# A windowed-attention and gated-MLP kernel on one core: VectorE takes values ahead of the next pair's mask, queries are turned between two output rows, later pairs are cast one slot sooner

## The chip, the core and the metric

The kernel runs on one core of a Trainium2 chip. A core has five engines that run side by side and meet only at semaphores: TensorE (PE in the profile; PEld is its weight load), VectorE (DVE), ScalarE (ACT), GpSimd (POOL) and SyncE (SP), which here only issues transfers. Each engine takes its instructions strictly in the order in which the program gives them. The metric is the device time of one execution in microseconds, the median of several runs.

## What is computed

Four batches, eight heads, 768 positions, head size 64. Attention with a window of 128 positions and four sink positions, then a gated MLP over the 512 joined head outputs, with a mixing over positions:

```python
scores = scale * np.matmul(q, k.transpose(0, 1, 3, 2))
is_sink = pos[None, :] < int(n_sink)
rel = pos[:, None] - pos[None, :]
in_window = (rel >= 0) & (rel < int(window))
scores = np.where(is_sink | in_window, scores, -1000000000.0)
a = np.exp(scores - np.max(scores, axis=-1, keepdims=True))
a = a / (np.sum(a, axis=-1, keepdims=True) + 1e-09)
x = np.matmul(a, v)            # then heads joined: (4, 768, 512)
...
h = x @ w_in                   # 512 -> 1024, then gelu (tanh form)
u, v = h[..., :512], h[..., 512:]
v_n = (v - mu) / np.sqrt(var + 1e-06) * g_ln
v_s = np.einsum('ts,bsd->btd', w_sg, v_n) + b_sg[None, :, None]
out = x + (u * v_s) @ w_out
```

## The kernel before

The work is cut into 16 pairs of heads (`n` = 0 to 15, four to a batch) and, behind each batch's four pairs, one MLP block. For a pair, `load` (L90) brings `k`, `q` and `v` from HBM, `cast` (L101) turns them to bf16 on GpSimd, and keys and queries are turned so that the head size lies on the partitions: `columns` (L215) does it by TensorE into PSUM with a copy out by ScalarE or VectorE, `columns_by_dma` (L228), for pairs 12 to 15, by transposing transfers on SP's queue.

`score(n, g)` (L251) computes the scores of group `g`, two of the six key tiles, in PSUM, and ScalarE's exponential writes them to `ex`. `keep_band` (L283) then zeroes what lies outside the window: for group 0 VectorE multiplies with a mask (L290), for groups 1 and 2 GpSimd runs two selects (L298, L300). `values(n, c)` (L307) multiplies half `c` of the pair's query tiles (three each) with the values and the sinks (L324, L330); VectorE then takes the reciprocal of the sums (L332) and the product that writes `x` (L333). `turn_x` (L337) turns `x` by TensorE, `turn_x_by_dma` (L352) by a transfer on SP.

The block of a batch is `hidden` (L577): six `hidden_v` units (L370, L377, gelu L379, statistics L381), eight `hidden_u` units (L389, L392), the inverse root, and the normalisation (L422). Steps of the next pair are placed between its units by unit number. What follows it in the MLP is put in the list `fillers`: eight gate units `spatial` (L424: six matmuls L432, then VectorE's L435 and L438) and six output rows `project` (L458: four matmuls L463; either VectorE adds `x` at L466, or a fifth matmul does at L469 and ScalarE copies at L472; then a store on SP). `fill()` takes the next unit off this list, so that TensorE has MLP work of the last batch between the attention steps of the next.

All PSUM tiles but the scores come from `bank` (L209), four buffers that go round: a tile waits until the tile four before it has been read out. Scores have two buffers of their own. The bf16 keys and queries have two buffers each, the raw loads three.

The order of all this is written by hand. For pairs 4 to 15 a loop (L701 to L760) writes it: slot `n` of the loop holds the scores and masks of pair `n`, the values of pair `n-1`, the turns of pair `n+1` and the casts of pair `n+2`, with conditions for the first slots, the last ones and those with a block (`block`, n = 8 and 12). In a slot, the mask of group 0 stands ahead of `values(n - 1, 0)`:

```python
        keep_band(n, 0, V)
        keep_band(n, 1, G)
        if n + 2 >= FIRST:
            cast_all(n + 2, "kq")
        if todo:
            values(n - 1, 0)
        fill(2 if n > HP and not todo else 1)
```

After a block no values of the pair before are left to do (`todo` is false), and the last thing placed inside it is `score(n + 1, 0, 1)` and two units of `fillers`. What follows the loop (from L761), the last pair's values and the last block, is the same in both kernels.

Of the kernel before, what the change touches and what calls it, by code (L numbers as in the profile page):

```python
# [18 lines left out]
def kernel(  # L19
# [14 lines left out]
    nc = tc.nc  # L34
# [317 lines left out]
    def turn_x_by_dma(n):  # L352
        b, hp = divmod(n, HP)
        nc.sync.dma_start_transpose(
            out=xT[b][:, hp, :].rearrange("c (t p) -> c t p", t=NT),
            in_=x_sb[b][:, hp].rearrange("p t c -> p (t c)"))
# [98 lines left out]
                A.copy(o_sb, o_ps[:, 0:m])  # L455
            (nc.sync if eng is V else A).dma_start(out=out[b, rows, cols], in_=o_sb)

    def project(b, t, by_act):  # L458
        rows = slice(128 * t, 128 * (t + 1))
        o_ps = bank([128, 512], F32, "o_ps")  # L460
        o_sb = small.tile([128, DM], F32, name="o_sb", bufs=6)
        for c in range(KU):
            nc.tensor.matmul(o_ps, gTs[b][:, c, rows], w_out_sb[:, c, :],  # L463
                             start=(c == 0), stop=(c == KU - 1 and not by_act))
        if not by_act:
            V.tensor_add(o_sb.rearrange("p (h d) -> p h d", h=HP),  # L466
                         o_ps.rearrange("p (h d) -> p h d", h=HP), x_sb[b][:, :, t, :])
        else:
            nc.tensor.matmul(o_ps.rearrange("p (h d) -> p h d", h=HP), iden, x_sb[b][:, :, t, :],  # L469
                             start=False, stop=True)  # L470
        if by_act:
            A.copy(o_sb, o_ps)  # L472
        nc.sync.dma_start(out=out[b, rows, :], in_=o_sb)


    LEAST, MOST = 1e-20, 1e20
# [95 lines left out]
    def fill(count=1):  # L572
        for _ in range(count):
            if fillers:
                fillers.pop(0)()

    def hidden(b, between):  # L577
        units = [lambda j=j: hidden_v(b, j) for j in range(NT)]
        units += [lambda f=f, n=n: hidden_u(b, f, n) for n in range(2) for f in range(KU)]
        after = {NT + 1: [lambda: inverse_root(b)]}  # L580
        for j in range(NT):
            after.setdefault(NT + 1 + j, []).append(lambda j=j: normalise(b, j))
        for i, unit in enumerate(units):
            unit()
            for step in after.get(i, []) + between.get(i, []):
                step()
        gate = [[lambda f=f, n=n: spatial(b, f, n) for f in range(KU)] for n in range(2)]
        if b < B - 1:
            fillers.extend(gate[0] + gate[1])
            order = (0, 2, 4, 1, 3, 5) if b < B - 2 else (1, 0, 2, 3, 4, 5)  # L590
            fillers.extend(lambda t=t: project(b, t, t % 2 == 1) for t in order)
# [98 lines left out]
    cast_all(HP + 1)  # L690
    load_w_out()

    QUOTA = {4: 3, 5: 3, 6: 3, 7: 2, 8: 1, 9: 3, 10: 3, 11: 3, 12: 3, 13: 3, 14: 3, 15: 3}
    LAST = NT + 2 * KU - 1

    def x_by_dma(n):
        return n >= 2 * HP and n % HP < HP - 2

    later = {2 * HP: (FIRST, FIRST + 1), 3 * HP: (NP - 1, NP)}
    valued = HP - 1  # L700
    for n in range(HP, NP):  # L701
        todo = valued < n - 1
        block = n % HP == 0 and n > HP
        if HP < n <= 2 * HP:
            load_all(n + 3)
        if n not in exps:
            score(n, 0, 1)
        if n == HP:
            for si in range(3, NT):
                turn_weights(si, V)  # L710
        keep_band(n, 0, V)
        keep_band(n, 1, G)
        if n + 2 >= FIRST:
            cast_all(n + 2, "kq")
        if todo:
            values(n - 1, 0)
        fill(2 if n > HP and not todo else 1)
        if n + 1 < FIRST and not block:
            columns(n + 1, "k", A)
            if not todo and n > HP:  # L720
                columns(n + 1, "q", V)
        if n == HP:
            columns(n + 1, "q", V)
            fill()
        score(n, 2)
        keep_band(n, 2, G)
        if todo:
            values(n - 1, 1)
            if x_by_dma(n - 1):
                turn_x_by_dma(n - 1)  # L730
        if FIRST <= n + 2 < NP:
            columns_by_dma(n + 2)
            if n + 4 == FIRST + 2:
                load_all(n + 4)
        if QUOTA[n] > 2 and todo:
            fill()
        if HP < n < FIRST - 1 and not block and todo:
            columns(n + 1, "q", A)
        if n + 2 <= NP:
            cast_all(n + 2, "v" if n + 2 >= FIRST else "kqv")  # L740
        if n == NP - 1:
            draw_gelu()
        if QUOTA[n] > 1:
            fill()
        if block:
            open_v(n // HP - 1, 0)
            open_v(n // HP - 1, 1)
        if todo and not x_by_dma(n - 1) and n < NP - 1:
            turn_x(n - 1, V)
        if block:  # L750
            open_v(n // HP - 1, 2)
        valued = n - 1
        if block:
            hidden(n // HP - 1, {1: [lambda: values(n, 0)], 3: [lambda: values(n, 1)],
                                 5: [lambda: columns(n + 1, "k", A)] if n + 1 < FIRST else [],
                                 6: [lambda m=m: load_all(m) for m in later.get(n, ())],
                                 7: [lambda: columns(n + 1, "q", A)] if n + 1 < FIRST else [],
                                 9: [lambda: turn_x_by_dma(n) if x_by_dma(n) else turn_x(n, V)],
                                 LAST: [lambda: score(n + 1, 0, 1), lambda: fill(2)]})
            valued = n  # L760
    values(NP - 1, 0)  # L761
    fill()
    turn_x(NP - 2, A)
# [51 lines left out]
```

## Time and profile before

| | us |
|---|---|
| median of 3 runs | 167.05 |
| the runs | 165.91, 167.05, 175.5 |
| profiled execution | 166.5 |
| its span, first to last instruction | 164.7 |
| TensorE busy | 153.1 |
| VectorE busy | 132.9 |
| ScalarE busy | 110.1 |
| GpSimd busy | 77.6 |

The span is what the profile's rows add up to; the profiled execution's own time has some 2 us around it. In rows of the timeline the columns are: start, length, engine, line, operation, output from inputs, count, and in brackets the idle time of the engine before it with what ended it. In rows of the chain of waits: start, length, engine and tile. The ends of matmuls are modelled, so overlapping lengths are usual there. The granted TensorE clock was full (0.991 in the mean).

The stages in time: pairs 0 to 3 to about 24 us, the first block to about 37, slots 4 to 8 to about 63.7, the second block to 76, slots 9 to 12 to 99.5, the third block to 111, slots 13 to 15 and the last pair's values to 130.7, then the last block, gate and rows.

### The profile page before, as it was taken

Reading aid. Unit: us, or ns where it says so; the run is one execution under the profiler, and the core shown is the slowest. Engines: PE = TensorE matmul, PEld = TensorE weight load, DVE = VectorE, ACT = ScalarE, POOL = GpSimd, SP = SyncE. Lnnn points to the kernel's source line nnn. Section 1 sums busy time; section 2 is a strip of 40 time slices with the busy share of each in tenths; the row PEclk is TensorE's granted clock in tenths of the full one; section 3 lists DMA queues with packets and bytes.
Section 4 is the critical chain, followed back from the end, with each engine's and each line's share of the span. In section 5 each row is a group of like instructions: output and inputs, shape, how many; then the busy total and the mean of one; then the engine's idle time right before and its main releaser. Section 6 shows DMA issues by size and latency. Waiting matters only on the chain.

```text
span 164.7 us, 4433 instructions
## 1 busy us (share of the span) xinstructions
PE 153.1 (93%) x1737; PEld 91.4 (55%) x1755; DVE 132.9 (81%) x321; ACT 110.1 (67%) x150; POOL 77.6 (47%) x113
## 2 busy tenths in 40 slices
PE   3999999999999999999999989999999999999950
PEld 3555574666566665564666645555565545455530
DVE  6787995996899986799889995989899869987520
ACT  3189878879978689698887466679759267411220
POOL 6568771207799989400289997000996000000000
PEclk9999999999999999999999999999999999999996
DMA  4999989999999999999902999999622310040361
GB/s 133 333 339 259 197 116 261 224 325 307 295 237 304 254 306 359 278 213 222 183 27 56 149 234 183 242 228 211 190 53 48 127 68 0 17 174 4 127 235 38
DMA packets 60195, 31.11 MB, mean 189 GB/s; under 512 B 48356, under 2 KB 57080, under 8 KB 60168
## 3 DMA queue, kind: packets, MB, share of 16 engines
q1 hardware_dynamic: 56800, 27.47, 70.5%
q0 software_dynamic: 2944, 2.77, 10.4%
q10 hardware_dynamic: 424, 0.53, 1.0%
q8 instruction: 15, 0.25, 0.6%
q14 instruction: 12, 0.10, 0.2%
HBM read 24.81 MB, written 6.29 MB: 189 GB/s over the span
## 4 chain that ended last, share of the span: by engine, by line
PE 68%; DVE 22%; issue 3%; ACT 2%; POOL 1%; DVEq 0%; ACTq 0%
PE vs L432 11%; PE hu L389 10%; PE o_ps L463 9%; PE hv L370 8%; PE sc L267 7%; PE av L324 6%; DVE gv L435 4%; DVE gT L438 3%; PE kps L219 3%; PE xps L341 3%; PE qps L219 2%; PE hv L377 2%; DVE st L381 2%; ACT ex L281 2%; PE av L330 2%
## 5 line engine op out<-in xcount | busy, mean ns | idle before, releaser
L281 ACT ACTIVATE ex<-sc 128x1024 bf16<-128x1024 f32 x48 | 47.5, 1025 | 11.8 <-PE sc L267 7.1
L432 PE MATMUL vs<-wsgT,vn 128*128 128x384 bf16 x192 | 35.3, 326 | 0.1
L298 POOL TENSOR_SCALAR_AFFINE_SELECT ex<-ex 128x512 bf16<-128x512 bf16 x24 | 16.8, 700 | 30.0 <-ACT ex L281 15.6
L463 PE MATMUL o_ps<-w_out_sb,gT 128*128 128x512 bf16 x83 | 22.9, 380 | 1.1 <-DVE x L333 0.6
L432 PEld LDWEIGHTS <-vn 128*128 128x128 bf16 x192 | 17.6, 98 | 10.8 <-DVE vn L422 0.2
L389 PE MATMUL hu<-xT,w_in_sb 128*128 128x384 bf16 x128 | 22.1, 326 | 0.0
L435 DVE SCALAR_TENSOR_TENSOR gv<-vs,g_sb,b_bc 128x384 bf16<-128x384 f32 x32 | 19.5, 610 | 2.5 <-PE vs L432 2.1
L381 DVE BATCH_NORM_STATS2 st<-v_all 128x6 f32<-128x512 f32 x24 | 16.1, 671 | 3.5 <-ACT v_all L379 3.5
L370 PE MATMUL hv<-w_in_sb,xT 128*128 128x512 bf16 x68 | 18.6, 379 | 0.3
L333 DVE TENSOR_TENSOR x<-av,rcps 128x384 bf16<-128x384 f32 x32 | 17.8, 558 | 1.1
L379 ACT ACTIVATE v_all<-hv 128x512 f32<-128x512 f32 x24 | 13.2, 599 | 7.8 <-PE hv L377 6.6
L392 ACT ACTIVATE uT<-hu 128x384 bf16<-128x384 f32 x32 | 15.7, 491 | 4.1 <-PE hu L389 3.7
L438 DVE TENSOR_TENSOR gT<-gv,uT 128x384 bf16<-128x384 bf16 x32 | 16.6, 517 | 2.2 <-DVE gv L435 0.5
L107 POOL CAST k_bf<-k_sb 128x768 bf16<-128x768 f32 x15 | 12.8, 853 | 11.1 <-DMA k_sb<-in_k_dram 5.8
L472 ACT COPY o_sb<-o_ps 128x512 f32<-128x512 f32 x13 | 7.4, 593 | 15.2 <-PE o_ps L469 7.5
L389 PEld LDWEIGHTS <-w_in_sb 128*128 128x128 bf16 x128 | 12.3, 98 | 8.0
L267 PE MATMUL sc<-qT,kT 64*128 64x256 bf16 (+2 forms) x384 | 16.0, 256 | 0.7 <-DVE qT L225 0.3
L107 POOL CAST q_bf<-q_sb 128x768 bf16<-128x768 f32 x15 | 14.4, 958 | 4.2 <-DMA q_sb<-in_q_dram 3.9
L324 PE MATMUL av<-v_sb,ex 128*128 128x65 bf16 x352 | 16.2, 194 | 0.0
L104 POOL CAST v_sb<-v_sb 128x768 bf16<-128x768 f32 x16 | 14.6, 911 | 3.0 <-DMA v_sb<-in_v_dram 2.9
L290 DVE TENSOR_TENSOR ex<-ex,mask 128x1024 bf16<-128x1024 bf16 x15 | 13.9, 925 | 2.5 <-ACT ex L281 2.3
L324 PEld LDWEIGHTS <-ex 128*128 128x128 bf16 x352 | 13.1, 97 | 4.7 <-issue 1.4
(90 smaller groups left out, 221.3 us busy)
## 6 DMA issues: line engine op xcount, KB each, us to landing
k_sb<-in_k_dram SPq DMA_DIRECT2D x16, 384.0 KB, 6.7
v_sb<-in_v_dram SPq DMA_DIRECT2D x16, 384.0 KB, 6.0
out_dram<-o_sb SPq DMA_DIRECT2D x23, 256.0 KB, 2.4
q_sb<-in_q_dram SPq DMA_DIRECT2D x15, 384.0 KB, 5.5
wsg_sb<-in_moe_w_sg_dram POOLq DMA_DIRECT2D x2, 576.0 KB, 11.3
w_in_sb<-in_moe_w_in_dram POOLq DMA_DIRECT2D x2, 256.0 KB, 5.1
w_in_sb<-in_moe_w_in_dram POOLq DMA_DIRECT2D x1, 512.0 KB, 5.4
w_out_sb<-in_moe_w_out_dram POOLq DMA_DIRECT2D x1, 512.0 KB, 9.2
```

The source lines that it names most:

```text
L107: eng.tensor_copy(dst.rearrange("p t (h d) -> p h t d", h=2), src)
L267: nc.tensor.matmul(sc[part, 512 * l + w:512 * l + w + n_q], kT[rows, 128 * j + wide * a:128 * j + wide * (a + 1)], qT[rows, 128 * j:128 * ...
L281: A.activation(out=exps[n][:, g, :], in_=sc, func=AF.Exp, scale=scale)
L324: nc.tensor.matmul(av[:, m, l, :], probs(j, l, half), v_sb[:, l, j, :], start=first, stop=False)
L333: V.tensor_mul(x_sb[b][:, hp, HT * c:HT * (c + 1), :].rearrange("p i (l d) -> p i l d", l=2), av[:, :, :, 0:64], rcp.to_broadcast([128, HT ...
L370: nc.tensor.matmul(hvs[b, j], xT[b][:, c, 128 * j:128 * (j + 1)], w_in_sb[:, c, DF:], start=(c == 0), stop=False)
L381: V.bn_stats(out=st, in_=v_alls[b][:, j, :])
L389: nc.tensor.matmul(h_ps[:, 0:NH], w_in_sb[:, c, 128 * f:128 * (f + 1)], xT[b][:, c, NH * n:NH * (n + 1)], start=(c == 0), stop=(c == KD - 1))
L432: nc.tensor.matmul(vs[:, 0:NH], vns[b][:, si, 128 * f:128 * (f + 1)], wsgT[:, si, cols], start=(si == 0), stop=(si == NT - 1))
L435: V.scalar_tensor_tensor(out=gv, in0=vs[:, 0:NH], scalar=g_sb[:, f:f + 1], in1=b_bc[:, cols], op0=ALU.mult, op1=ALU.add)
L438: V.tensor_mul(gTs[b][:, f, cols], gv, uTs[b][:, f, cols])
L463: nc.tensor.matmul(o_ps, gTs[b][:, c, rows], w_out_sb[:, c, :], start=(c == 0), stop=(c == KU - 1 and not by_act))
```

## The change

The loop is replaced by a list of steps in the order in which they are emitted. A letter names the function: `S` scores, `m` masks (`m 5 0 1`: groups 0 and 1 of pair 5), `A0`/`A1` the halves of `values`, `ck cq cv` casts, `KA QA KV QV` turns of keys or queries with the engine of the copy, `TD` turns by transfer, `XV XA XD` turns of `x`, `L` loads, `F` a unit of `fillers`, `W` weights, `O` the opening of `hidden_v`, `B` a block. Most of the list repeats the loop's order. What differs:

- In slots 5, 6, 7, 10, 11, 14 and 15, `A0` of the pair before stands ahead of the mask of group 0 (and of group 1, which runs on another engine).
- Slot 8: the mask of group 0 of pair 8 stands behind both halves of pair 7's values. The output row between them is split: its matmuls stay (`D`), its ScalarE copy and its store (`E`) come behind `A1`, and so behind the exponentials of group 2. `project` gets the argument `ends` for it.
- Slot 12: the mask of group 0 of pair 12 stands behind both halves of pair 11's values and the output row after them.
- Behind the second block: the queries of pair 10 are turned between the two output rows and not three units later; the casts of pair 11's keys and queries and pair 10's values stand ahead of pair 9's group 1 and 2 selects.
- The key and query casts of pairs 12, 13 and 14 stand at the end of slots 9, 10 and 11 and not between the selects of slots 10, 11 and 12; the key cast of pair 15 stands ahead of the selects of pair 13.

```diff
-    def project(b, t, by_act):
+    def project(b, t, by_act, ends=None):
...
-        if not by_act:
-            V.tensor_add(o_sb.rearrange("p (h d) -> p h d", h=HP),
-                         o_ps.rearrange("p (h d) -> p h d", h=HP), x_sb[b][:, :, t, :])
-        else:
+        if by_act:
             nc.tensor.matmul(o_ps.rearrange("p (h d) -> p h d", h=HP), iden, x_sb[b][:, :, t, :],
                              start=False, stop=True)
-        if by_act:
-            A.copy(o_sb, o_ps)
-        nc.sync.dma_start(out=out[b, rows, :], in_=o_sb)
+        def end():
+            if by_act:
+                A.copy(o_sb, o_ps)
+            else:
+                V.tensor_add(o_sb.rearrange("p (h d) -> p h d", h=HP),
+                             o_ps.rearrange("p (h d) -> p h d", h=HP), x_sb[b][:, :, t, :])
+            nc.sync.dma_start(out=out[b, rows, :], in_=o_sb)
+        if ends is None:
+            end()
+        else:
+            ends.append(end)
...
-    for n in range(HP, NP):
-        todo = valued < n - 1
-        block = n % HP == 0 and n > HP
...
+    INSIDE = {
+        1: {1: "A0 8", 3: "A1 8", 5: "KA 9", 6: "L 12, L 13", 7: "QA 9", 9: "XD 8",
+            LAST: "ck 11, cq 11, cv 10, S 9 0 1, F 1, QV 10, F 1"},
+        2: {1: "A0 12", 3: "A1 12", 6: "L 15, L 16", 9: "XD 12", LAST: "S 13 0 1, F 2"},
+    }
+    ORDER = """
+        S 4 0 1, W 3 4 5, m 4 0 1, F 1, KA 5, QV 5, F 1, S 4 2, m 4 2, ck 6, cq 6, cv 5, F 1,
+        L 8, S 5 0 1, A0 4, m 5 0 1, F 1, KA 6, S 5 2, m 5 2, A1 4, F 1, QA 6,
+        ck 7, cq 7, cv 6, F 1, XV 4,
+        L 9, S 6 0 1, A0 5, m 6 0 1, F 1, KA 7, S 6 2, m 6 2, A1 5, F 1, QA 7,
+        ck 8, cq 8, cv 7, F 1, XV 5,
+        L 10, S 7 0 1, A0 6, m 7 0 1, F 1, KA 8, S 7 2, m 7 2, A1 6, QA 8,
+        ck 9, cq 9, cv 8, F 1, XV 6,
+        L 11, S 8 0 1, A0 7, m 8 1, D, S 8 2, m 8 2, A1 7, E, m 8 0, ck 10, cq 10, cv 9,
+        O 1 0, O 1 1, XV 7, O 1 2, B 1,
+        m 9 0 1, F 1, KA 10, F 1, S 9 2, m 9 2, ck 12, cq 12, F 1,
+        S 10 0 1, A0 9, m 10 0 1, F 1, KA 11, S 10 2, m 10 2, A1 9, XD 9, TD 12, L 14,
+        F 1, QA 11, cv 11, ck 13, cq 13, F 1,
+        S 11 0 1, A0 10, m 11 0 1, F 1, S 11 2, m 11 2, A1 10, TD 13, F 1, cv 12, ck 14, cq 14,
+        F 1, XV 10,
+        S 12 0 1, A0 11, m 12 1, F 1, S 12 2, m 12 2, A1 11, TD 14, F 1, m 12 0, cv 13, F 1,
+        O 2 0, O 2 1, XV 11, O 2 2, B 2,
+        ck 15, m 13 0 1, cq 15, F 2, S 13 2, m 13 2, TD 15, cv 14, F 1,
+        S 14 0 1, A0 13, m 14 0 1, F 1, S 14 2, m 14 2, A1 13, XD 13, F 1, cv 15, F 1,
+        S 15 0 1, A0 14, m 15 0 1, F 1, S 15 2, m 15 2, A1 14, F 1, G, F 1
+    """
...
+    run(ORDER)
```

The function `run` only calls, for each letter, the function named above; `D` calls `fillers.pop(0)(ends)` and `E` calls `ends.pop()()`. The step `B` calls `hidden` with the entries of `INSIDE` as what is placed between its units.

More of the change, by code (lines that the diff above doesn't have):

```diff
@@ L589, in hidden @@
             fillers.extend(gate[0] + gate[1])
+            by_act = (1, 3, 5)
             order = (0, 2, 4, 1, 3, 5) if b < B - 2 else (1, 0, 2, 3, 4, 5)
-            fillers.extend(lambda t=t: project(b, t, t % 2 == 1) for t in order)
+            fillers.extend(lambda ends=None, t=t: project(b, t, t in by_act, ends) for t in order)
             return
@@ L691 @@
     load_w_out()
-    QUOTA = {4: 3, 5: 3, 6: 3, 7: 2, 8: 1, 9: 3, 10: 3, 11: 3, 12: 3, 13: 3, 14: 3, 15: 3}
     LAST = NT + 2 * KU - 1
[L696 to L700, printed above, removed]
-    for n in range(HP, NP):
-        todo = valued < n - 1
-        block = n % HP == 0 and n > HP
[L704 to L760, printed above, removed]
```

40 lines of the change are left out of this document (added).

## The prediction

> **What bounds the kernel now.** I read the page's busy shares and the shares of the chain of waits first, then the windows, then the timeline of every slot that the change touches.
>
> ```profile
> PE 153.1 (93%) x1737; PEld 91.4 (55%) x1755; DVE 132.9 (81%) x321; ACT 110.1 (67%) x150; POOL 77.6 (47%) x113
> PE 68%; DVE 22%; issue 3%; ACT 2%; POOL 1%; DVEq 0%; ACTq 0%
> 43.50:130.70 87.20, 85.63 (x1076) 51.97 (x1085) 77.17 (x182) 65.71 (x87) 54.50 (x77) 1.00 0.94 198
> ```
>
> TensorE carries the chain, VectorE takes it over for a fifth. The edits lie between 43.5 us (scores of pair 5) and 130.7 us (the last pair's values). The third row is that stretch: its length, then the busy time of PE, PEld, DVE, ACT and POOL. TensorE is idle there for 87.20 - 85.63 = 1.57 us. The change takes no matmul away and adds none, so what it can win is this idle time, and a little that the modelled ends of stalled matmuls hide: some 2 us in all, about 1.2% of 166.5 us. Before 43.5 us nothing changes; after 130.7 us the order is the old one and only shifts. The question is thus which stalls of TensorE go, one by one. In all that follows I compare the starts of successive matmul groups, since their ends are modelled.
>
> **Values ahead of the mask: slot 7.** In slots 5 to 7, 10, 11, 14 and 15 the reciprocal and product of `values(n-1, 0)` now stand ahead of the mask of pair n, group 0, on VectorE. No other engine's order changes by that. The PSUM tiles of `bank` go round in four buffers, so the product that empties one lets the fourth tile after it start. In slot 7 that tile is `qps` (queries of pair 8).
>
> ```profile
> 52.69 0.34 PE L330 MATMUL av<-vsink,ex 128*128 128x195 bf16 x2
> 52.90 0.50 PE L432 MATMUL vs<-wsgT,vn 128*128 128x384 bf16 x2
> ...
> 57.08 0.99 DVE L290 TENSOR_TENSOR ex<-ex,mask 128x1024 bf16<-128x1024 bf16 x1
> 58.21 0.56 DVE L333 TENSOR_TENSOR x<-av,rcps 128x384 bf16<-128x384 f32 x1
> 58.45 0.34 PE L330 MATMUL av<-vsink,ex 128*128 128x195 bf16 x2
> 58.91 0.50 PE L219 MATMUL qps<-iden,q_bf 128*128 128x128 bf16 x6
> ```
>
> Unhindered, the next group starts 52.90 - 52.69 = 0.21 us after the sink matmuls; here it takes 58.91 - 58.45 = 0.46, because the product ended at 58.77. Without the mask's 0.99 ahead of it, it ends near 57.8. **Gain 0.25.** The mask then ends some 0.8 us later; its reader is the same pair's `values`, a whole slot (over 5 us) away, so that costs nothing.
>
> **Slot 9: queries of pair 10 turned between the two output rows.**
>
> ```profile
> 78.68 2.11 PE L432 MATMUL vs<-wsgT,vn 128*128 128x384 bf16 x12
> 79.69 1.08 ACT L472 COPY o_sb<-o_ps 128x512 f32<-128x512 f32 x2
> 79.88 0.64 POOL L298 TENSOR_SCALAR_AFFINE_SELECT ex<-ex 128x512 bf16<-128x512 bf16 x1 [11.96 <-ACT ex L281]
> 80.63 0.50 PE L219 MATMUL kps<-iden,k_bf 128*128 128x128 bf16 x6
> 80.96 0.50 PE L219 MATMUL qps<-iden,q_bf 128*128 128x128 bf16 x6
> 81.39 0.36 PE L267 MATMUL sc<-qT,kT 64*32 64x256 bf16 x16
> 81.74 1.15 PE L432 MATMUL vs<-wsgT,vn 128*128 128x384 bf16 x6
> 82.15 0.95 DVE L225 COPY qT<-qps 128x768 bf16<-128x768 bf16 x1
> 83.16 0.61 PE L267 MATMUL sc<-qT,kT 64*128 64x256 bf16 x8 [0.27 <-DVE qT L225]
> ```
>
> One gate unit is (80.63 - 78.68)/2 = 0.98 us, so the scores of pair 10 could have started at 81.74 + 0.98 = 82.72. They start at 83.16: 0.44 lost to the copy of `qT`, queued on VectorE behind two gate units. After the change that copy runs before them. What is late next is the keys' turn (`kps`): it now follows one gate unit instead of two, would start at 78.68 + 0.33 (the queries' turn, 80.96 - 80.63) + 0.98 = 79.99, and takes the PSUM buffer of the first output row, which ScalarE copies out until 79.69 + 0.54 = 80.23. From there: 0.33 for the turn, 0.98 for a gate unit, 0.35 for score group 2 (81.74 - 81.39), 0.98 for the next unit: 82.87, or about 82.9 with the hand-overs. **Gain 0.26**; 0.44 if ScalarE is earlier, none if it is 0.3 later.
>
> **Casts one slot sooner.** The casts of pair 11's keys and queries and of pair 10's values go ahead of slot 9's selects, into the 11.96 us in which GpSimd waits (row of 79.88): three casts of under 1 us each, which need only loads issued in slot 8 and buffers freed by the turns inside the block. Their cost is taken as nothing; if they ran later, against the normalisation, the cover would be the fraction of a microsecond between its end and the first gate unit. The other two pairs move from between the selects of groups 1 and 2 to behind group 2, which frees group 2's selects:
>
> ```profile
> 85.90 0.47 PE av L324 x12
> 91.17 0.60 PE av L324 x12
> ...
> 90.59 0.86 POOL L300 TENSOR_SCALAR_AFFINE_SELECT ex<-ex 128x256 bf16<-128x256 bf16 x1
> ```
>
> In the chain, the second half of pair 10's values takes 0.60 against 0.47 a slot before, since the selects it reads end at 91.45. **Gain 0.13.** On SP the transposes of pair 12 and behind them the loads of pair 14 issue up to a microsecond sooner; nobody waits for them in the trace. For pair 15 only the key cast moves ahead of a select, again in idle GpSimd time: 0.
>
> **Slot 12: the mask of group 0 behind both halves and a row's addition.**
>
> ```profile
> 56.60 0.86 PE o_ps L463 x4
> ...
> 96.10 0.82 POOL L104 CAST v_sb<-v_sb 128x768 bf16<-128x768 f32 x1
> 96.26 1.20 DVE L290 TENSOR_TENSOR ex<-ex,mask 128x1024 bf16<-128x1024 bf16 x1
> 96.83 1.02 PE L463 MATMUL o_ps<-w_out_sb,gT 128*128 128x512 bf16 x3
> 97.60 0.56 DVE L333 TENSOR_TENSOR x<-av,rcps 128x384 bf16<-128x384 f32 x1
> 98.22 1.04 PE L463 MATMUL o_ps<-w_out_sb,gT 128*128 128x512 bf16 x4 [0.36 <-DVE x L333]
> ```
>
> The row started at 96.83 needs 0.86 (chain), so the next could start at 97.69; it waits for the product's buffer until 98.22: 0.53. With the mask's 1.20 gone from ahead of it the product ends near 97.1. **Gain 0.53.** The mask then runs near 99, two microseconds before the pair's values.
>
> **Slots 14 and 15.**
>
> ```profile
> 118.12 0.22 PE L330 MATMUL av<-vsink,ex 128*128 128x65 bf16 x2
> 118.82 0.96 DVE L290 TENSOR_TENSOR ex<-ex,mask 128x1024 bf16<-128x1024 bf16 x1 [0.46 <-ACT ex L281]
> ...
> 127.26 0.56 DVE L333 TENSOR_TENSOR x<-av,rcps 128x384 bf16<-128x384 f32 x1
> 127.87 1.04 PE L463 MATMUL o_ps<-w_out_sb,gT 128*128 128x512 bf16 x4 [0.21 <-DVE x L333]
> ```
>
> VectorE is idle 0.46 us for the exponentials although the values are done at 118.34, and then works without a pause. With the values first it starts that much sooner, and the product at 127.26 with it. **Gain 0.21.**
>
> **Slot 8: the one place with a price.** A projection's matmuls stay, its ScalarE copy and the store on SP move behind score group 2's exponentials (the store has only loads behind it that are cast two slots later), and the mask moves behind both products.
>
> ```profile
> 62.08 0.69 DVE L290 TENSOR_TENSOR ex<-ex,mask 128x1024 bf16<-128x1024 bf16 x1 [0.61 <-ACT ex L281]
> 63.97 0.56 DVE L333 TENSOR_TENSOR x<-av,rcps 128x384 bf16<-128x384 f32 x1
> 64.60 0.63 POOL L298 TENSOR_SCALAR_AFFINE_SELECT ex<-ex 128x512 bf16<-128x512 bf16 x1
> 65.36 0.62 DVE L350 COPY xT<-xps 128x384 bf16<-128x384 bf16 x2 [0.84 <-PE xps L341]
> ...
> L290 DVE TENSOR_TENSOR ex<-ex,mask 128x1024 bf16<-128x1024 bf16 x15 | 13.9, 925 | 2.5 <-ACT ex L281 2.3
> ```
>
> The mask, free at 64.53, ends at 65.22 if it takes 0.69, and at 65.73 if it takes the 1.20 seen at 96.26; from 65.36 on it delays the copy of `xT`, for which the block waits. That is 0 to 0.37; by the mean of 0.925 it is **0.10 lost**, which I take, since selects run beside it. At 96.26 the mask met a cast that ran until 96.92 and came out 0.51 longer than alone. The Trainium skill, "SBUF — State Buffer", section "Who interferes with whom", has it that a VectorE instruction with two SBUF inputs and a GpSimd one reading SBUF exclude each other, the later waiting for all of the earlier; the trace agrees roughly, 0.51 for a remaining 0.66. By that rule a select that starts first, at 64.60, would hold the mask to 65.23 and the copy to 65.92, and the sum would be 0.46 worse.
>
> **The sum.** 0.25 + 0.26 + 0.13 + 0.53 + 0.21 - 0.10 = 1.28. The profiled execution took 166.5 us (span 164.7), so 166.5 - 1.3 = 165.2. The runs shown are 165.91, 167.05 and 175.5: 166.5 is the middle of the first two, and their median lies 0.55 above it.
>
> **The rivals.**
>
> *Stalls come back elsewhere.* Freed buffers only let TensorE run into the next wait, ScalarE's copies in slot 9 and VectorE's unbroken work from 118.8 to 127.8. Then slots 9 and 14 to 15 give nothing, and slot 8 takes its 0.37: 166.5 - (0.25 + 0.13 + 0.53) + 0.37 = 166.0. For it: VectorE is busy for 77.17 of 87.20 us. Against it: the waits removed are waits on VectorE's order, not its load.
>
> *A load stands ahead of a select (the slower side).* On GpSimd, the casts of pair 14 now stand ahead of pair 12's first selects, and these casts need loads issued in slot 10.
>
> ```profile
> 92.90 0.65 SPq L95 DMA_DIRECT2D q_sb<-in_q_dram  x1
> DMA to landing us min/median/max: 4.6/5.4/5.6
> 102.01 0.47 PE L324 MATMUL av<-v_sb,ex 128*128 128x65 bf16 x10
> 95.00:100.00 5.00, 4.59 (x59) 2.20 (x57) 4.93 (x10) 2.96 (x4) 5.00 (x8) 1.00 1.63 201
> ```
>
> The queries of pair 14 are issued at 92.90, or about 1.3 sooner now, and land 5.4 later: near 97.0. A cast (0.85) and two selects (1.3) end near 99.2 to 100; the values that read them start at 102.01, or 100.9 with TensorE 1.1 sooner. The slack is about 1 us. From a landing of 6.4 us on TensorE waits, and past 7.7 the gain is spent. If the crowded DMA engines (share 1.63 there) double it to 10.8, the wait is 4.4 and the time 166.5 - 1.3 + 4.4 = 169.6. Against it: no query load in this trace took over 5.6.
>
> *More comes free than the stalls counted.* GpSimd was full from 85 to 100 us (5.00 of 5) and is relieved; with the mask shorter beside fewer casts, all 1.57 us of idle time go, and as much again of stretched matmuls: 166.5 - 3.1 = 163.4. Against it: the chain shows most matmul groups at their usual length.
>
> **How the numbers follow.** Forecast 0.62, stalls elsewhere 0.16, load ahead of the select 0.09, more free 0.13. The range reaches from 163.4, the third rival, to the second's 166.0 with the first two runs' half-distance of 0.57 and the load's first microsecond on it, 167.5. Two per cent (3.3 us, about what a measurement of this kernel can tell from no change) asks for less than 163.2 or more than 169.8. Faster by that: half of the last rival's chance (its better half, 0.065) and as much from the forecast with a lucky median, together 0.12. Slower: half of the load's chance (0.045) and a small rest, 0.06. Within: 0.82.
>
> **What would show it.** In the new profile the waits of `o_ps` for the product `x` and of `sc` for `qT` should be gone from TensorE's list, `kps` in slot 9 should wait for ScalarE's copy, GpSimd's 11.96 us of idle time should hold three casts, and slots 7, 9, 11 and 12 should be shorter by the terms above. The prediction is wrong if a select of pair 12 starts behind an idle GpSimd, if the block after slot 8 waits for `xT`, or if the slots shorten and the last 34 us grow.

## The result and the profile after

| | before | after |
|---|---|---|
| median of 7 runs, us | 167.05 | 165.46 |
| profiled execution, us | 166.5 | 165.46 |
| its span, us | 164.7 | 163.7 |
| ratio of the times, 95% interval | | 0.9944 [0.9919, 0.9969] |

The ratio leaves out the executions of 172 us and more, three of seven before and one of seven after; the others took 165.91 to 167.05 and 165.22 to 165.6. The change gains about half a per cent: measurably something, and well within 2%. On another chip, in a later comparison, the same kernel gave 0.9936 [0.9915, 0.9957]. The prediction was 165.2, 0.26 below the median measured. What is to be learnt lies in its terms.

First the page of the changed kernel: busy time of each engine, the engines' shares of the chain that ended last, and the group of VectorE's mask products (count, busy time, mean ns).

```profile
PE 153.3 (94%) x1755; PEld 90.8 (55%) x1755; DVE 130.8 (80%) x321; ACT 110.2 (67%) x150; POOL 78.6 (48%) x113
...
PE 74%; DVE 15%; DMA 4%; issue 2%; POOL 1%; ACT 1%; SPq 0%; DVEq 0%; ACTq 0%
```

```profile
L290 DVE TENSOR_TENSOR ex<-ex,mask 128x1024 bf16<-128x1024 bf16 x15 | 11.9, 794 | 0.0
```

The windows row from the scores of pair 5 to the opening of the last block (length, then busy time of PE, PEld, DVE, ACT, POOL), and then the whole list of TensorE's waits (who waited, for whom, us, times, longest):

```profile
43.60:129.60 86.00, 85.83 (x1085) 51.93 (x1085) 76.60 (x182) 65.82 (x87) 55.72 (x77) 1.00 0.96 201
```

```profile
PE warm L149 <- POOL iden masks.py:199: 2.8, 1, 2.8
PE sc L267 <- DVE qT L225: 0.4, 1, 0.4
PE kps L219 <- POOL k_bf L107: 0.3, 1, 0.3
PE av L324 <- POOL v_sb L104: 0.2, 1, 0.2
```

VectorE's share of the chain fell from 22% to 15%. The stretch fell from 87.20 to 86.00 us, and what the row counts as TensorE's idle time from 1.57 us to 86.00 - 85.83 = 0.17. Not all of the 1.57 was idle, though. In these slots the trace of the kernel before lacks ten matmul records, seven of `o_ps` and three of `hv` (the row at 96.83 in the prediction has three of its four), and each leaves a gap of 0.05 us. Some 1.05 us was idle time. All four waits in the list lie before 18.5 us, where nothing was changed: in the rest of the trace TensorE waits for nobody for as much as the list counts. The mask products became shorter as well, 13.9 us in all to 11.9; but 1.1 of that lies ahead of 24 us, where nothing was changed. From slot 5 on they went from 9.39 to 8.56: four of the eleven are longer than 0.70 there, each started with 0.30 us or more of a GpSimd cast or select still to run, where it was six.

Three stretches of the changed kernel's timeline, in slots 7, 9 and 12 (start, length, engine, line, operation, output from inputs, count):

```profile
57.52 0.56 DVE L333 TENSOR_TENSOR x<-av,rcps 128x384 bf16<-128x384 f32 x1
58.00 0.68 DVE L290 TENSOR_TENSOR ex<-ex,mask 128x1024 bf16<-128x1024 bf16 x1
...
78.88 0.95 DVE L225 COPY qT<-qps 128x768 bf16<-128x768 bf16 x1
...
79.70 1.08 ACT L472 COPY o_sb<-o_ps 128x512 f32<-128x512 f32 x2
...
79.99 0.50 PE L219 MATMUL kps<-iden,k_bf 128*128 128x128 bf16 x6
...
98.27 1.24 POOL L107 CAST q_bf<-q_sb 128x768 bf16<-128x768 f32 x1 [0.94 <-DMA q_sb<-in_q_dram]
99.47 0.63 POOL L298 TENSOR_SCALAR_AFFINE_SELECT ex<-ex 128x512 bf16<-128x512 bf16 x1
```

The product of slot 7 ends at 58.08, not 58.77. The copy of `qT` of pair 10 runs at 78.88, not 82.15. The pair 14 cast does wait for its load, 0.94 us, with pair 12's selects behind it; they end in time all the same, for no wait of TensorE follows.

To see where the microsecond came from, take the start of each pair's first scores from the timeline. A slot is the time from there to the next pair's, and slot 15 ends where the last block opens (`hv`):

```
slot                      7      8      9     10     11     12     13   14+15
before                 5.03  15.43   7.19   5.60   5.29  17.02   6.18   13.23
after                  4.84  15.46   6.87   5.60   5.26  16.49   6.38   12.84
difference            -0.19  +0.03  -0.32   0.00  -0.03  -0.53  +0.20   -0.39
predicted             -0.25  +0.10  -0.26   0.00  -0.13  -0.53   0.00   -0.21
```

The differences add up to -1.23. Pair 4 started 0.14 later in this execution, ahead of all edits, and another 0.12 went behind the last slot: about -1.0 in the span. The terms predicted add up to -1.28, but slot 13 has another sign than forecast, and slots 14 and 15 make up for it.

In slot 13 the wait list shows nothing, but the gate units became longer. The changed kernel's timeline there, with the same columns (the second is the length):

```profile
109.67 0.17 DVE L416 SCALAR_TENSOR_TENSOR y<-s,y 128x6 f32<-128x6 f32 x1
109.73 0.83 POOL L107 CAST k_bf<-k_sb 128x768 bf16<-128x768 f32 x1 [7.29 <-DMA k_sb<-in_k_dram]
109.87 0.71 DVE L414 TENSOR_TENSOR s<-y 128x6 f32<-128x6 f32 x1
110.61 0.17 DVE L415 TENSOR_TENSOR s<-s,h 128x6 f32<-128x6 f32 x1
...
111.01 2.83 DVE L422 TENSOR_SCALAR vn<-v_all,mv,y 128x512 bf16<-128x512 f32 x6
...
112.89 2.32 PE L432 MATMUL vs<-wsgT,vn 128*128 128x384 bf16 x12
```

Lines 414 to 416 are the steps of the inverse root: 128x6 values, 0.17 us each. One of them took 0.71, and it ended at 110.58, when pair 15's key cast on GpSimd did (109.73 + 0.83 = 110.56). The normalisation `vn`, for which the gate units wait, starts that much later, and 12 gate matmuls take 2.32 us where two units otherwise take 1.96 to 2.1.

### The profile page after: what moved, and what is told of

It is laid out like the page before. It is cut to its first block, busy times and chain, and to the rows that moved or that the text cites. A ratio compares the mean times of both kernels' runs of the same rounds, so it can differ in the third digit from the quotient of the medians.

```text
span 163.7 us, 4451 instructions
## 1 busy us (share of the span) xinstructions
PE 153.3 (94%) x1755; PEld 90.8 (55%) x1755; DVE 130.8 (80%) x321; ACT 110.2 (67%) x150; POOL 78.6 (48%) x113
## 4 chain that ended last, share of the span: by engine, by line
PE 74%; DVE 15%; DMA 4%; issue 2%; POOL 1%; ACT 1%; SPq 0%; DVEq 0%; ACTq 0%
PE vs L432 15%; PE o_ps L464 10%; PE hu L389 10%; PE hv L370 8%; PE av L324 7%; PE sc L267 7%; DMA v_sb<-in_v_dram 4%; PE hv L377 3%; PE kps L219 2%; PE xps L341 2%; DVE st L381 2%; PE av L330 2%; PE qps L219 2%; DVE vsink L160 2%; DVE gv L435 2%
## 5 line engine op out<-in xcount | busy, mean ns | idle before, releaser
L298 POOL TENSOR_SCALAR_AFFINE_SELECT ex<-ex 128x512 bf16<-128x512 bf16 x24 | 17.9, 745 | 14.4 <-ACT ex L281 10.6
L438 DVE TENSOR_TENSOR gT<-gv,uT 128x384 bf16<-128x384 bf16 x32 | 15.2, 475 | 2.2 <-DVE gv L435 0.5
L104 POOL CAST v_sb<-v_sb 128x768 bf16<-128x768 f32 x16 | 13.6, 853 | 3.8 <-DMA v_sb<-in_v_dram 3.7
L300 POOL TENSOR_SCALAR_AFFINE_SELECT ex<-ex 128x512 bf16<-128x512 bf16 (+1 forms) x24 | 13.8, 574 | 0.0
```

What stands on the lines that cost most here:

```text
L298: eng.affine_select(out=diag, in_=diag, compare_op=ALU.is_ge, fill=0.0, base=0, pattern=[[0, 2], [0, 2], [1, 128]], channel_multiplier=-1)
```

## The experiments

All of them start from the changed kernel. e1 to e9 and e11 ran once each. Two profiles of the changed kernel, on two chips, have spans of 163.7 and 162.9, and the 0.8 between them lies ahead of slot 4 and behind slot 15 alone. So the slots are compared. With the same order in them they repeat to 0.05 us; slot 11, slot 13 and slot 6 (not in the table, 5.82 to 6.21) vary more, and the text comes to the first two:

```
slot                               7      8      9     10     11     12     13   14+15   10 to 12
before                          5.03  15.43   7.19   5.60   5.29  17.02   6.18   13.23      27.91
after                           4.84  15.46   6.87   5.60   5.26  16.49   6.38   12.84      27.35
e1_mask_first                   5.03  15.42   6.87   5.87   6.12  16.48   6.37   12.99      28.47
e2_slot12                       4.85  15.47   6.87   5.60   5.15  16.48   6.40   12.84      27.23
e3_q10_late                     4.84  15.47   7.19   5.61   6.07  16.48   6.36   12.83      28.16
e4_k15_late                     4.84  15.45   6.87   5.60   5.16  16.48   6.18   12.84      27.24
e5_slot8                        4.85  15.43   6.86   5.61   5.15  16.48   6.36   12.84      27.24
e6_casts_late                   4.85  15.45   6.87   5.84   5.82  16.48   6.18   12.84      28.14
e7_k15_q15_early                4.85  15.44   6.87   5.60   5.49  16.47   7.00   12.84      27.56
e8_q10_late_t12_first           4.85  15.47   7.19   5.61   5.22  16.48   6.48   12.84      27.31
e9_k15_late_t12_first           4.85  15.46   6.87   5.60   5.48  16.48   6.18   12.84      27.56
e10_k15_t12_k6                  4.85  15.46   6.87   5.60   5.15  16.48   6.19   12.84      27.23
e11_old_order_10_12_t12_first   4.85  15.45   6.87   5.76   5.85  16.48   6.19   12.84      28.09
e12_changed_again               4.84  15.45   6.87   5.60   5.19  16.48   6.49   12.84      27.27
```

### Pair 15's key cast back behind the mask step (e4_k15_late)

```diff
-        ck 15, m 13 0 1, cq 15, F 2,
+        m 13 0 1, ck 15, cq 15, F 2,
```

> Only the key cast of pair 15 goes back behind the group 1 selects of pair 13. Theory (a GpSimd cast that is running holds up one of VectorE's small operations of the inverse root, which took 0.71 us and not 0.17, and so the normalisation and the first gate units behind the third block): that operation is back at 0.17, the normalisation starts 0.55 sooner against the block's scores, slot 13 goes from 6.38 to 6.18 us, span 0.2 shorter. Rival (slot 13 is longer since the block ran earlier against ScalarE's or SP's work): slot 13 stays at 6.3 to 6.4.

Slot 13 went back to 6.18, and 164.88 us were taken (span 163.1). The timeline of this kernel at the same two lines:

```profile
109.50 0.17 DVE L414 TENSOR_TENSOR s<-y 128x6 f32<-128x6 f32 x1
...
110.10 2.83 DVE L422 TENSOR_SCALAR vn<-v_all,mv,y 128x512 bf16<-128x512 f32 x6
```

No step of the root is held up any more, and slot 13 has the length it had before. The whole loss of slot 13 belongs to this one cast.

### Two casts in the same place (e7_k15_q15_early)

```diff
-        ck 15, m 13 0 1, cq 15, F 2,
+        ck 15, cq 15, m 13 0 1, F 2,
```

> Doubled cost: both casts of pair 15 stand ahead of pair 13's selects. Theory (a running cast holds up VectorE's small operations and, if it meets it, the normalisation): the second cast follows the first or waits for its load, which is issued about 0.5 to 1 us after the first's, so it runs near 111 us beside the normalisation; if that is held too, slot 13 grows from 6.38 to 6.6 to 6.9 us, and if the normalisation does not take part, it stays at 6.4. Rival (no holding up): 6.18 to 6.4 and no operation longer than usual.

Slot 13 took 7.00. Its timeline:

```profile
117.61 0.83 POOL L107 CAST k_bf<-k_sb 128x768 bf16<-128x768 f32 x1 [7.52 <-DMA k_sb<-in_k_dram]
117.62 0.83 DVE L414 TENSOR_TENSOR s<-y 128x6 f32<-128x6 f32 x1
...
119.42 0.83 POOL L107 CAST q_bf<-q_sb 128x768 bf16<-128x768 f32 x1 [0.98 <-DMA q_sb<-in_q_dram]
119.49 3.31 DVE L422 TENSOR_SCALAR vn<-v_all,mv,y 128x512 bf16<-128x512 f32 x6
...
121.25 2.92 PE L432 MATMUL vs<-wsgT,vn 128*128 128x384 bf16 x12
```

The key cast holds a step of the root for its full 0.83, and the query cast stretches the normalisation from 2.83 to 3.31. Extra work 0.66 + 0.48 = 1.14, growth of the slot 7.00 - 6.18 = 0.82. In the changed kernel it was 0.71 - 0.17 = 0.54 and 0.20, in e12 0.64 and 0.31: each time some 0.33 us go into slack and TensorE pays the rest. That is the price of this step. The row of e12, once more an operation of the root beside the key cast:

```profile
109.38 0.81 DVE L414 TENSOR_TENSOR s<-y 128x6 f32<-128x6 f32 x1
```

The Trainium skill, "SBUF — State Buffer", section "Who interferes with whom", says that of a VectorE and a GpSimd instruction that need the ports they share, the later waits for the whole of the earlier; in the changed kernel the held step ends 0.02 us behind the cast, in e7 0.01, so the trace agrees.

The total of this run, 174.96 us, is not comparable: in its profile, and in that of e10, one VectorE product at the start of slot 5 took several microseconds (last section).

### Slot 12's mask back in its old place (e2_slot12)

```diff
-        S 12 0 1, A0 11, m 12 1, F 1,
+        S 12 0 1, m 12 0 1, A0 11, F 1,
...
-        TD 14, F 1, m 12 0, cv 13, F 1,
+        TD 14, F 1, cv 13, F 1,
```

> Only slot 12 is put back: pair 12's mask of group 0 ahead of pair 11's values. Theory: the fourth PSUM tile waits for the product behind the mask again, slot 12 with its block goes from 16.49 back to about 17.0 us. Rival (the mask was slow, 1.20 us, only because a cast ran beside it, and in the new order of casts it takes 0.7): half or less of it comes back, under 16.75.

Slot 12 stayed at 16.48; 165.41 us. Its timeline, and behind it one row of the kernel before:

```profile
93.76 0.68 DVE L474 TENSOR_TENSOR o_sb<-o_ps,x 128x512 f32<-128x512 f32 x1
...
95.30 0.69 DVE L290 TENSOR_TENSOR ex<-ex,mask 128x1024 bf16<-128x1024 bf16 x1 [0.39 <-ACT ex L281]
...
96.13 0.56 DVE L333 TENSOR_TENSOR x<-av,rcps 128x384 bf16<-128x384 f32 x1
96.45 1.89 PE L464 MATMUL o_ps<-w_out_sb,gT 128*128 128x512 bf16 x8
```

```profile
95.19 0.68 DVE L466 TENSOR_TENSOR o_sb<-o_ps,x 128x512 f32<-128x512 f32 x1
```

The mask is ahead of the product again, and the eight matmuls of the two output rows run without a gap. Counted from the slot's start (93.67 here, 94.05 before), the row's addition ran at 0.09, and at 1.14 before; the mask started at 1.63 and took 0.69, and before it started at 2.21 and took 1.20. So VectorE came into slot 12 late in the kernel before and then met a cast. The 0.53 us were won by the edits that bring VectorE and GpSimd into this slot earlier, and the edit to which the prediction gave them is worth nothing beside those. What that edit alone would have won in the kernel before was not tried.

### Masks ahead of values again (e1_mask_first)

In slots 5, 6, 7, 10, 11, 14 and 15, as here:

```diff
-        A0 6, m 7 0 1,
+        m 7 0 1, A0 6,
```

> The masks of group 0 stand ahead of the first half of the values again in slots 5, 6, 7, 10, 11, 14 and 15; all else as in the changed kernel. Slot lengths are between the first score matmuls of successive pairs. Theory (VectorE's order sets when PSUM buffers come free): slot 7 goes from 4.84 back to 5.03 us, slots 14 and 15 with the last values from 12.84 to 13.23, the others stay within 0.05; span about 0.55 longer. Rival (the relief of GpSimd by the earlier casts made these slots shorter): both stay within 0.05, span unchanged.

166.79 us, span 165.0. Slot 7 went back to 5.03, so its gain of 0.19 is this edit's. Of the gain in slots 14 and 15 only 0.15 of 0.39 was lost. But slots 10 to 12 took 28.47, more than the 27.91 of the kernel before. The timeline at the end of slot 11:

```profile
93.39 0.56 DVE L333 TENSOR_TENSOR x<-av,rcps 128x384 bf16<-128x384 f32 x1
94.01 0.34 PE L341 MATMUL xps<-iden,x 128*128 128x128 bf16 x3 [0.52 <-DVE x L333]
...
94.56 0.61 PE L267 MATMUL sc<-qT,kT 64*128 64x256 bf16 x8 [0.21 <-DMA qT<-q_bf]
```

Two waits that the kernel before does not show: the turn of `x` waits for VectorE's product, and the scores of pair 12 wait for a transfer.

### Queries of pair 10 late again (e3_q10_late)

```diff
-            LAST: "ck 11, cq 11, cv 10, S 9 0 1, F 1, QV 10, F 1"},
+            LAST: "ck 11, cq 11, cv 10, S 9 0 1, F 2"},
...
-        m 9 0 1, F 1, KA 10, F 1, S 9 2,
+        m 9 0 1, F 2, KA 10, QV 10, S 9 2,
```

> Only pair 10's queries are turned behind pair 10's keys again, the casts stay early. Theory: slot 9 goes from 6.87 back to 7.1 to 7.2 us, the scores of pair 10 waiting for the copy of qT; and since VectorE's normalisation ends 0.55 us later in the changed kernel, the first gate unit, now 0.33 earlier on TensorE, may wait for it too, up to 0.2 more: 7.4. Rival (the early casts shortened slot 9): stays at 6.9.

166.38 us, span 164.7. Slot 9 is back at 7.19, so the 0.32 there is this edit's. Slot 11 grew by 0.81 on top. This kernel's timeline, with SP's transposing transfers of `x` of pair 9 and of keys and queries of pair 12 (SPq is SP issuing):

```profile
82.81 0.61 PE L267 MATMUL sc<-qT,kT 64*128 64x256 bf16 x8 [0.28 <-DVE qT L225]
...
87.90 1.22 SPq L354 DMA_TRANSPOSE xT<-x  x1
...
89.30 2.18 SPq L233 DMA_TRANSPOSE kT<-k_bf  x1
...
91.57 1.24 SPq L233 DMA_TRANSPOSE qT<-q_bf  x1
...
94.49 0.61 PE L267 MATMUL sc<-qT,kT 64*128 64x256 bf16 x8 [0.78 <-DMA qT<-q_bf]
```

The old wait for `qT` from VectorE is there again (first row, 0.28), and then comes a chain that no row of the wait list of either kernel shows. SP issues the transfers in order; the first needs VectorE's product of pair 9's second half, and each takes 1.2 to 2.2 us. The scores of pair 12 start 94.49 - (91.57 + 1.24) = 1.68 us after the last issue ends. The changed kernel, same view:

```profile
87.20 1.22 SPq L354 DMA_TRANSPOSE xT<-x  x1
...
88.60 1.21 SPq L233 DMA_TRANSPOSE kT<-k_bf  x1
...
89.91 2.11 SPq L233 DMA_TRANSPOSE qT<-q_bf  x1
```

There the last issue ends at 92.02 and the scores start at 93.69, 1.67 later: it was at this limit, with no listed wait to tell of it. In e2, e4 and e5, where the last issue took 1.78 to 1.90 and not 2.11, the scores start 1.78 to 1.92 after its end, and slot 11 is 5.15: they were no longer waiting. So the limit cost the changed kernel 0.11 (0.04 in e12, where slot 11 took 5.19). In the kernel before the last issue ended at 92.22 and the scores started at 94.05, 1.83 later, with 0.16 to spare.

### Pair 12's transfers ahead of x's (e8_q10_late_t12_first)

The edits of e3, and on SP pair 12's transfers first:

```diff
-        A1 9, XD 9, TD 12, L 14,
+        A1 9, TD 12, XD 9, L 14,
```

> As the run with pair 10's queries turned late, but on SP's queue the two transposing transfers of pair 12's keys and queries stand ahead of that of pair 9's x. In that run slot 11 had grown from 5.26 to 6.07 us, TensorE waiting for the transferred qT. Theory (SP's queue holds pair 12's transfers behind x of pair 9, which waits for VectorE's product): they go out 1 us or more sooner, slot 11 is back at 5.15 to 5.3 us, slot 9 stays at 7.19. Rival (the transfers wait for the casts or for the DMA engines): slot 11 stays at 5.8 or more.

165.93 us. Slot 9 stayed at 7.19, and slot 11 went back from 6.07 to 5.22. SP in its timeline:

```profile
86.10 1.22 SPq L233 DMA_TRANSPOSE kT<-k_bf  x1
87.41 1.24 SPq L233 DMA_TRANSPOSE qT<-q_bf  x1
88.73 1.24 SPq L354 DMA_TRANSPOSE xT<-x  x1
```

`kT` no longer stands behind VectorE's product. So what e3 lost in slot 11 came by way of SP's queue, where pair 12's transfers stood behind a late product of VectorE, and not from VectorE or GpSimd holding up TensorE themselves.

### All casts late again (e6_casts_late)

The casts of pairs 10 to 15 stand where they stood before, for instance:

```diff
-        S 10 2, m 10 2, A1 9, XD 9, TD 12, L 14, F 1, QA 11, cv 11, ck 13, cq 13, F 1,
-        S 11 0 1, A0 10, m 11 0 1, F 1, S 11 2, m 11 2,
+        S 10 2, m 10 0 1, ck 12, cq 12, m 10 2, A1 9, XD 9, TD 12, L 14, F 1, QA 11, cv 11, F 1,
+        S 11 0 1, A0 10, m 11 0 1, ck 13, cq 13, F 1, S 11 2, m 11 2,
```

> All casts of pairs 10 to 15 are put back to the places of the kernel before; the orders of VectorE and the early turn of pair 10's queries stay. In the run with pair 12's mask put back, slot 12 kept its 16.48 us, so the mask's place was not what shortened it from 17.02. Theory A (VectorE is less far behind when slot 12 begins, because values stand ahead of masks in slots 10 and 11 and the copy of qT is done before slot 9): slot 12 stays at 16.5. Theory B (casts that ran beside VectorE's two-input operations made them longer): slot 12 goes back to 16.9 or more. Both expect slot 13 back at 6.18, since no cast runs beside the inverse root.

165.65 us. Slots 10 and 11 lost 0.24 and 0.56, slot 13 won its 0.20 back, slot 12 stayed. Its timeline up to the start of slot 12:

```profile
88.30 0.94 POOL L107 CAST k_bf<-k_sb 128x768 bf16<-128x768 f32 x1
...
89.26 2.27 SPq L233 DMA_TRANSPOSE kT<-k_bf  x1
...
94.54 0.61 PE L267 MATMUL sc<-qT,kT 64*128 64x256 bf16 x8 [0.60 <-DMA qT<-q_bf]
```

The same transfers as in e3. This time that of `kT` starts when pair 12's key cast ends, 88.30 + 0.94 = 89.24, and takes 2.27 to issue. Taking back any one of the three, the order of values and masks, pair 10's queries or the casts, makes slots 10 to 12 longer than they were before; with SP's order as it stands, only all three together win.

### VectorE's old order, with the transfer chain cut (e11_old_order_10_12_t12_first)

Masks ahead of values in slots 10 and 11 as in e1, slot 12 as in e2, and SP's order as in e8.

> In slots 10, 11 and 12 VectorE's order is that of the kernel before (masks ahead of values), the casts and the early turn of pair 10's queries stay, and pair 12's transfers stand ahead of that of pair 9's x, so that no scores wait for them. Theory (slot 12 was long because VectorE came into it about 1 us behind; where it was short with the old orders, TensorE had waited in slot 11 for the transferred qT and VectorE had caught up): slot 11 stays under 5.5 us and slot 12 grows to 16.8 to 17.1. Rival (casts or masks beside one another decide): slot 12 stays at 16.5 with slot 11 under 5.5.

165.53 us. Slots 10 to 12 took 28.09, of which slot 12 was an unchanged 16.48: the stall was expected in slot 12 and came in slot 11.

```profile
94.11 0.34 PE L341 MATMUL xps<-iden,x 128*128 128x128 bf16 x3 [0.53 <-DVE x L333]
```

With the transfers out of the way the old order of VectorE still costs 28.09 - 27.35 = 0.74 against the changed kernel. It shows at the first thing that needs VectorE, here the turn of `x` at the end of slot 11 (0.53, and the rest in slot 10); in the kernel before that was the output row of slot 12. Pair 15's key cast has its place from the changed kernel here, and yet slot 13 is 6.19:

```profile
108.19 0.83 POOL L107 CAST k_bf<-k_sb 128x768 bf16<-128x768 f32 x1 [7.65 <-DMA k_sb<-in_k_dram]
...
108.74 0.31 DVE L407 TENSOR_SCALAR w<-mv 128x6 f32<-128x6 f32 x1
```

The cast waits for its load, and here it landed so that the cast stretched one operation from 0.17 to 0.31. The extra 0.14 is below the slack of 0.33. So the price of that cast varies from run to run with the landing.

### Slot 8's edit undone (e5_slot8)

```diff
-        S 8 0 1, A0 7, m 8 1, D, S 8 2, m 8 2, A1 7, E, m 8 0,
+        S 8 0 1, m 8 0 1, A0 7, F 1, S 8 2, m 8 2, A1 7,
```

> Only slot 8 is put back: pair 8's mask of group 0 ahead of pair 7's values, the output row's copy by ScalarE ahead of the exponentials of group 2. Theory (the moved mask costs the copy of xT a little, and the split row gains nothing since no PSUM tile was waited for there): slot 8 with its block goes from 15.46 to 15.42 us, span the same within 0.1. Rival (the order of slot 8 pays further on, through GpSimd's earlier selects or the earlier exponentials): the block or slot 9 gets longer by 0.2 or more.

165.41 us; slot 8 took 15.43 against 15.46, and no other slot moved beyond its spread. The edit is worth nothing either way.

### Towards a better version (e9, e10), and the changed kernel once more (e12)

e9 takes pair 15's key cast back (e4) and swaps SP's order (e8 without e3). e10 has pair 6's key cast moved ahead as well, by this edit on top of e9:

```diff
-        m 4 0 1, F 1, KA 5, QV 5, F 1, S 4 2, m 4 2, ck 6, cq 6,
+        m 4 0 1, ck 6, F 1, KA 5, QV 5, F 1, S 4 2, m 4 2, cq 6,
```

> The version of this call without the moved cast of pair 6: slot 5 at 6.18 us, slot 11 at 5.15, slot 13 at 6.18; the moved cast of pair 6 is worth the difference in slots 4 to 6, expected 0.2.

> A version meant to beat both kernels: the changed kernel with the key cast of pair 15 behind the group 1 selects of pair 13, with the two transfers of pair 12 ahead of that of pair 9's x on SP, and with the key cast of pair 6 between the selects of groups 1 and 2 of pair 4, since TensorE's turn of those keys waited for that cast in slot 5. Expected: slot 13 at 6.18 us, slot 11 at 5.15, slot 5 at 5.95 to 6.0 instead of 6.18; together 0.5 us less than the changed kernel, about 164.9. If GpSimd's casts meet VectorE's masks elsewhere because of the new places, a slot grows by 0.1 to 0.3 and the sum falls to 0.2.

> The changed kernel itself, timed again on the same chip as the version above, for the comparison: 165.2 to 165.6 us.

e9 took 164.72 us in its one execution, span 163.0. Slot 13 is 6.18, but slot 11 was 5.48 and not 5.15:

```profile
90.08 1.33 DVE L290 TENSOR_TENSOR ex<-ex,mask 128x1024 bf16<-128x1024 bf16 x1
...
93.46 0.34 PE L341 MATMUL xps<-iden,x 128*128 128x128 bf16 x3 [0.16 <-DVE x L333]
```

A mask beside casts took 1.33 instead of 0.68, and the product behind it came late. In e7, with the changed kernel's order, the same mask took 1.33 too and the slot 5.49; in e10, with e9's order, the slot took 5.15. Such a meeting comes and goes from one execution to the next.

e10 and e12 were timed against the same runs of the kernel before, on one chip (its median there 166.37):

| | ratio, 95% interval |
|---|---|
| e10_k15_t12_k6 | 0.9875 [0.9848, 0.9902] |
| e12_changed_again | 0.9936 [0.9915, 0.9957] |

The intervals do not overlap: e10 beats both kernels, by 1.2% the one before. The single executions that the two ratios rest on overlap all the same: 163.97 to 164.99 in e10 and 164.67 to 165.61 in e12, four of each. By the slots of its profile it gains 0.2 to 0.3 in slot 13 and up to 0.1 in slot 11 on the changed kernel's two profiles. The two ratios differ by 0.006 x 166.4 = 1.0 us, the medians of these executions by 0.7; where the rest comes from, and whether pair 6's cast has a part in it, the profile can't tell, since slot 5 is the one with the long product. That stays open.

## Why the prediction was right in total, and where its steps failed

The total agrees, -1.23 measured in the slots against -1.28, and in part by luck: slots 7, 11 and 13 came 0.06, 0.10 and 0.20 worse than forecast, slots 8, 9 and 14 to 15 came 0.07, 0.06 and 0.18 better.

- **Slot 7, 0.25 predicted, 0.19 measured.** Right, and e1 shows the cause: with the mask first, the slot is 5.03 again.
- **Slot 9, 0.26 predicted, 0.32 measured.** Right, and e3 shows it. The keys' turn started at 79.99, the time worked out for it without a wait for ScalarE's copy. The step "takes the PSUM buffer of the first output row" did not hold: ScalarE copied that row from 79.70 to about 80.3, and the first matmul of `kps` waits in the trace on a semaphore of VectorE alone. So at this place the four buffers did not go round in strict order. The whole stall went, and it was not 0.44: a gate unit ahead of scores takes 1.06 to 1.08 from start to start (80.34 to 81.40 and 81.75 to 82.83 in the changed kernel) and not 0.98, which leaves 83.16 - 81.74 - 1.08 = 0.34.
- **Slot 11, 0.13 predicted, 0.03 measured.** The step "nobody waits for them in the trace", said of pair 12's transposes, failed. True of the trace before, but these transfers were just in time: in the changed kernel the scores start 1.67 us after the last issue ends, as they do in e1, e3 and e6, where they visibly wait for it. Where the transfers were not at this limit (e2, e4, e5) the slot took 5.15, a gain of 0.14 on before. That this gain comes from group 2's selects, as the prediction has it, is not shown: no run takes those casts back alone.
- **Slot 12, 0.53 predicted, 0.53 measured, for another reason.** The step "with the mask's 1.20 gone from ahead of it" failed: with the mask put back (e2) nothing is lost, and it takes 0.69 there. The stall came from VectorE's late start into the slot and from the cast beside the mask; which of the two counts for more was not separated. e2, e6 and e11 all keep 16.48, so no single edit tried alone brings the stall back there; e1, e3, e6 and e11 show that the time lost appears in slots 10 and 11 instead.
- **Slot 13, 0 predicted, 0.20 to 0.31 lost.** The step "for pair 15 only the key cast moves ahead of a select, again in idle GpSimd time: 0" failed. GpSimd's time was idle, but VectorE's beside it was not: the cast holds a step of the inverse root. The prediction had looked at casts against the normalisation, with its one long operation, for the casts of slot 9, and not at the chain of 0.17 us steps ahead of it, nor at slot 13. e4 and e7 show the cause from both sides. The same happened in the changed kernel's second block (the two rows below), at no cost: e6, with these casts late, holds no step there, and its slots 8 and 9 are the same to 0.01.

```profile
73.03 0.83 POOL L104 CAST v_sb<-v_sb 128x768 bf16<-128x768 f32 x1
73.16 0.72 DVE L407 TENSOR_SCALAR w<-mv 128x6 f32<-128x6 f32 x1
```

- **Slots 14 and 15, 0.21 predicted, 0.39 measured.** The term was mis-sized. Values ahead of masks is worth 0.15 with the casts early (12.99 in e1, 12.84 after), and 0.39 with the casts late (13.23 before, 12.84 in e6, which has the casts of before). So the early casts alone would have given 0.24, and the values-first order takes that over. Which stall of those slots the casts shorten was not separated.
- **Slot 8, 0.10 lost predicted, 0.03 measured.** Within what a slot repeats to; e5 shows no price and no gain. The mask took 1.07 beside two selects (at 64.40), and the copy of `xT` started 0.61 us behind its turn instead of 0.53. That is about the delay forecast, but the block did not pass it on to TensorE.
- **The rivals.** "Stalls come back elsewhere" did happen, in slot 13 and at the limit of pair 12's transfers, but cost 0.3 and not 1. "A load stands ahead of a select": the cast did wait 0.94 for its load, and the selects behind it were still in time. "More comes free than the stalls counted": nearly all the idle time went, as that rival had it, but that was some 0.9 us and not 1.57, and of stretched matmuls another 0.3 came free and not as much again.

## What to carry to other kernels

A wait that is nought in a trace may be just about to bind: before calling a moved step free, work out how much later each transfer and each product could come, along the queue that issues it, and not only who waits now. Where several edits bring one engine forward into a slot, take each back alone before giving one of them the gain. And when a GpSimd instruction is moved into idle time, look at every VectorE instruction beside it, the tiny ones first: a step of 0.17 us paid up to 0.66 for a cast of 0.83.

## What the runs showed of the hardware

- A GpSimd cast of 0.83 us held 128x6 VectorE operations of 0.17 us for 0.31, 0.71, 0.81 and 0.83 us, by how much of the cast was left.
- In the 14 traces, 118 mask products and steps of the root start with more than 0.15 us of a GpSimd cast or select still to run. In 116 of them the growth is what was left, less 0.13 to 0.16 us: the mask at 52.24 in the changed kernel took 0.92 instead of 0.68, with 0.38 left of a cast. It goes the other way as well: the cast at 98.27 started 0.12 behind a mask of 0.68, and took 1.24 instead of 0.83.
- In the rows shown, SP took 1.21 to 2.27 us to issue one transposing transfer, and scores that waited for the last of three started 1.66 to 1.68 us after its issue had ended.
- In two profiled executions one VectorE product at the start of slot 5, 0.38 to 0.49 us long in the twelve others, took more than ten times that. The one in e10, with the load that GpSimd issued ahead of it:

```profile
41.52 0.78 POOL L196 DMA_DIRECT2D w_out_sb<-in_moe_w_out_dram  x1
...
43.28 5.53 DVE L438 TENSOR_TENSOR gT<-gv,uT 128x384 bf16<-128x384 bf16 x1
```

In e7 it was 7.42 us, at 44.09, again 1.8 us after that load's issue at 42.33. Slot 5 took 14.05 and 12.40 us there instead of 6.18, which accounts for the long totals of these two executions (174.96 and 170.66 us). The distance to the load is not the cause by itself: in e1, e4, e5, e6 and e11 the same product starts as far behind that issue (1.76 us) and takes 0.48 or 0.49. What the cause is stays open.
